# Standing PSUM banks for three projections, and two pieces of tile work placed one iteration later, in a fused attention and expert-lookup kernel

## The chip, the cores and the metric

The kernel runs on one core of one Trainium2 chip. The metric is device time in microseconds of one execution; the number for a kernel is the median of several executions. The core has five engines with a queue each: the Tensor engine (PE, with its weight loads shown apart as PEld), the Vector engine (DVE), the Scalar engine (ACT), GpSimd (POOL) and SyncE (SP), which here only issues DMAs. Each engine works through its own queue in program order; semaphores hold an instruction until what it needs is there.

## The reference

Two branches over the same 2048 tokens of width 512 (32 heads, 16 features) are mixed by a gate:

```python
# A: linear attention with a softmax feature map
qkv = (x @ wqkv)...                                  # q, k, v per head
pq, pk = q @ w_phi, k @ w_phi                        # per head, 16 x 16
phi_q = concat(softmax(pq), softmax(-pq)); phi_k likewise
kv = sum_s phi_k^T v;  z = sum_s phi_k
o = (phi_q @ kv) / (phi_q @ z + 1e-6);  a = o @ wo
# B: 256 experts as 16 x 16, the best one per head
q = x @ w_q;  s1 = q1 @ k1^T;  s2 = q2 @ k2^T        # 16 scores each
e = argmax(s1) * 16 + argmax(s2)                     # top 1, so its softmax is 1
b = sum_h gelu(x . u[e]) * v[e]
# gate
g = sigmoid(x . gate_w);  out = g * a + (1 - g) * b
```

## The kernel before, in words

The tokens are cut into 16 tiles of 128. A matmul of two float32 operands is made of three of a shorter type, high by high, high by low and low by high (`mm3`, lines 52 to 61; the matmuls of lines 57, 59, 60 and 61), over four blocks of the contraction, so twelve matmuls per projection.

Three projections of a tile have 512 columns of which the last 32 are exactly zero, because the last of the 16 features (or score rows) of every head was subtracted from all others: `pq`, the features of q (`front_q`), and `s`, the scores of the first and the second half (`front_s`, half 0 and 1). They are run with `rest=480`: the first matmul of a group writes all 512 columns, so that the 32 zero columns are in the bank, and the other eleven write 480. A fourth projection, `pp` (258 columns, `front_p`), gives the products with u and the gate.

PSUM has eight banks of 512 float32: four with the tag `mm` (`mm_bank`), which every projection, the output `po` of odd tiles and some small results are given in turn, three with the tag `tr` for transposed results, and one with the tag `acc`, first for the sums over k and v (`kvacc`), then for `po` of even tiles.

A first phase over the 16 tiles computes v and the softmax features of k and adds them up in `acc` (`vproj`, `kproj`, `kvacc`); it leaves the work of tiles 14 and 15 partly to the second phase. The second phase is written out by hand in the order in which each engine's queue gets it. Its loop (`for a in range(NT - 2)`, iterations 0 to 13) does for tile a, with the next tile n = a + 1 and older ones:

- PE: `pq` of a (`front_q`); the output of tile a-3 (`push`, `pop`: `po`, 18 matmuls of line 661); the mask of a (`mid_mask`, `mk`: eight small matmuls that read `et`); `oT` of a-2 (`mid_num`, reads `kvb`); both score halves of n; `pp` of n.
- DVE: the softmax of `pq` (lines 117 to 123), with steps of the expert counting woven in (`count`, lines 579 to 613; tile 15's steps come from `step(last, ...)`); sums (472, 476); `best` of n, the equality with the row maximum (lines 504 and 505), for each half.
- ACT: copies, exponentials of the softmax (`soft_exp`, line 462), transposition planes, the output's copy `ot` (line 684).
- GpSimd: products such as `w` (line 468).
- SP: `turn_eq` (line 511) transposes `eq` of n by DMA into `et`, which the mask of the next iteration reads.

In iteration 1 the loop also does both score halves of tile 15, v of tile 14, `best`, `et` and the mask of tile 15. In iteration 2 it does v of tile 15, ends the sums with `kvacc` of 14 and 15, copies them to `kvb` (`kv_final`, line 724), and splits the output weights wo into `wbh` (ACT, lines 820 and 825) and `wbl` (line 861, two blocks on DVE and two on GpSimd). After the loop come tiles 14 and 15, written out; the output of tile 15 goes in two halves through banks `poA` and `poB`.

Of the kernel before, what the change touches and what calls it, by code (L numbers as in the profile page):

```python
# [9 lines left out]
F32 = mybir.dt.float32  # L10
# [24 lines left out]
def mix_kernel(ctx, tc, xT, wqT, wkT, wv, wphi, wo, wq, kk, ug, ev, cst, out):  # L35
# [13 lines left out]
        act.copy(hi, src)  # L49
        eng.tensor_tensor(lo, src, hi, op=ALU.subtract)  # L50

    def mm3(o, pairs, first=True, last=True, rest=None):
        n = len(pairs)
        o_, r = o[:, :rest] if rest else o, slice(0, rest)
        for i, (ah, al, bh, bl) in enumerate(pairs):
            if first and i == 0:
                pe.matmul(o, ah, bh, start=True, stop=False)  # L57
            else:
                pe.matmul(o_, ah, bh[:, r], start=False, stop=False)  # L59
            pe.matmul(o_, ah, bl[:, r], start=False, stop=False)  # L60
            pe.matmul(o_, al, bh[:, r], start=False, stop=(last and i == n - 1))  # L61
# [43 lines left out]
        for k in range(NK):  # L105
            pe.matmul(o[:, :n], xs(t, k)[0], wl[:, k, c0:c0 + n], start=False, stop=(k == NK - 1))

    def proj(o, t, wh, wl, c0, c1, ks=range(NK), rest=None):
        mm3(o, [(*xs(t, k), wh[:, k, c0:c1], wl[:, k, c0:c1]) for k in ks], ks[0] == 0, ks[-1] == NK - 1, rest)

    by_head = lambda a: a.rearrange("p (f h) -> p h f", f=F)

# [146 lines left out]
        pool.tensor_tensor(cols(sl), t3, cols(sh), op=ALU.subtract)  # L259

    st8 = {t: {} for t in range(NT)}

    def front_s(t, half, ks=range(NK)):
        e = st8[t]
        if ks[0] == 0:
            e[half] = mm_bank(f"s{half}_{t}")
        if t == 0 and half == 1:
            return low_last(e[half], t, sh, sl, 512, NR)
        proj(e[half], t, sh, sl, 512 * half, 512 * half + 512, ks, rest=NR)

    pool.memset(warm, 0.0)
    tab = w1.tile([P, 1], F32, bufs=1, name="tab")
# [130 lines left out]
        while t in chains:  # L403
            step(t)

    def front_p(t, evict=True):
        pp = st8[t]["pp"] = mm_bank(f"pp{t}")
        proj(pp[:, :NU], t, uh, ul, 0, NU)
        if evict:
            gelu_pre(t)  # L410
# [29 lines left out]
        pool.tensor_tensor(px, x2, px, op=ALU.mult)  # L440

    def front_q(t):
        pq = mm_bank(f"pq{t}")
        proj(pq, t, wah, wal, 0, D, rest=NR)
        st8[t]["pq"] = pq

    def soft_in(t, step=lambda: None):
# [59 lines left out]

    def turn_eq(t):
        e = st8[t]
        e["et"] = w3.tile([P, 8, P], BF16, tag="eqT", bufs=1, name=f"et{t}")  # L510
        sp.dma_start_transpose(e["et"], e["eq"])

    def mid_phi(t):
# [57 lines left out]
    def count(t, o):  # L571
        e = st8[t]
        i = 2 if t == NT - 1 else t % 2
        A, B = sa[i], sb[i]
        bor = ALU.bitwise_or
        act.copy(A[:, :, 8:24], o.rearrange("p (g a) -> p g a", a=F))
        yield True
        yield True
        yield dve.tensor_tensor(B[:, :, 8:24], A[:, :, 8:24], A[:, :, 7:23], op=bor)
        yield dve.tensor_tensor(A[:, :, 8:24], B[:, :, 8:24], B[:, :, 6:22], op=bor)  # L580
        yield dve.tensor_tensor(B[:, :, 8:24], A[:, :, 8:24], A[:, :, 4:20], op=bor)
        yield dve.tensor_tensor(A[:, :, 8:24], B[:, :, 8:24], B[:, :, 0:16], op=bor)
        m1 = w3.tile([P, 32, 2], U16, tag="m1", name=f"m1{t}")
        m2 = w3.tile([P, 32], U16, tag="m2", name=f"m2{t}")
        twice = lambda a: a.unsqueeze(3).to_broadcast([P, 2, F, 2])
        dve.tensor_tensor(m1.rearrange("p (w a) j -> p w a j", a=F), twice(A[:, 0:2, 8:24]), twice(A[:, 0:2, 7:23]),
                          op=ALU.bitwise_xor)
        yield dve.tensor_tensor(m2.rearrange("p (w a) -> p w a", a=F), A[:, 2:4, 8:24], A[:, 2:4, 7:23],
                                op=ALU.bitwise_xor)
        if t == NT - 1:  # L590
            X = w4.tile([P, 2 * NX], U16, tag="Xl", bufs=1, name=f"X{t}")
        else:
            X = w3.tile([P, 2 * NX], U16, tag="X", bufs=1, name=f"X{t}")
        T = (w4 if t == NT - 1 else w3).tile([P, 2 * NX], U16, tag="Tl" if t == NT - 1 else "T", bufs=1, name=f"T{t}")
        x32, t32 = X.bitcast(U32), T.bitcast(U32)
        srl, band = ALU.logical_shift_right, ALU.bitwise_and
        m1w = m1.rearrange("p a b -> p (a b)").bitcast(U32).rearrange("p (w a) -> p w a", a=F)
        m2w = m2.bitcast(U32).rearrange("p (w b) -> p w b", b=8)
        yield dve.tensor_tensor(x32.rearrange("p (w a b) -> p w a b", w=2, b=8),
                                m1w.unsqueeze(3).to_broadcast([P, 2, F, 8]),  # L600
                                m2w.unsqueeze(2).to_broadcast([P, 2, F, 8]), op=band)
        yield dve.tensor_scalar(t32, x32, 1, 0x55555555, op0=srl, op1=band)
        yield dve.tensor_tensor(X, X, T, op=ALU.subtract)
        yield dve.tensor_scalar(t32, x32, 2, 0x33333333, op0=srl, op1=band)
        yield dve.tensor_single_scalar(x32, x32, 0x33333333, op=band)
        yield dve.tensor_tensor(X, X, T, op=ALU.add)
        yield dve.tensor_tensor(T[:, :NX], X[:, :NX], X[:, NX:], op=ALU.add)
        yield dve.tensor_scalar(x32[:, :NX // 2], t32[:, :NX // 2], 4, 0x0F0F0F0F, op0=srl, op1=band)
        yield dve.tensor_single_scalar(t32[:, :NX // 2], t32[:, :NX // 2], 0x0F0F0F0F, op=band)
        yield dve.tensor_tensor(X[:, :NX], X[:, :NX], T[:, :NX], op=ALU.add)  # L610
        e["C"] = T.bitcast(F32) if t == NT - 1 else w3.tile([P, NX], F32, tag="cf", name=f"cf{t}")
        x8 = X[:, :NX].bitcast(U8).rearrange("p (n b) -> p n b", b=2)
        yield dve.tensor_tensor(e["C"], x8[:, :, 0], x8[:, :, 1], op=ALU.add)
# [19 lines left out]
        act.copy(ch, tj)  # L633
        e["c"] = (ch, cl, tj)

    def back_c(t):
        e = st8[t]
        o = mm_bank(f"CT{t}")
        for j in range(2):
            pe.matmul(o[:, j * P:(j + 1) * P], e["C"][:, j * P:(j + 1) * P], ident, start=(j == 0), stop=(j == 1),  # L640
                      is_transpose=True, skip_group_check=True)
        ch = w4.tile([P, 2 * P], F32R, tag="ch", name=f"ch{t}")
        cl = w4.tile([P, 2 * P], F32R, tag="cl", name=f"cl{t}")
        act.copy(ch, o[:, :2 * P])
        e["c"] = (ch, cl, o)
# [4 lines left out]

    queue, ended = [], []

    def push(t, low_last=False):
        e, h = st8[t], {}

        def mm(lhs, rhs, first=False, last=False):
            def go():
                if first:
                    h["po"] = e["po"] = (psum.tile([P, 512], F32, tag="acc", name=f"po{t}") if t % 2 == 0 else
                                         mm_bank(f"po{t}"))  # L660
                pe.matmul(h["po"], lhs(), rhs, start=first, stop=last)  # L661
                if last:
                    ended.append(t)
            return go
# [108 lines left out]
    def dealt(a, b, z):  # L773
        def first():
            for _ in gate(a):
                step(b)
            step(b, 4)
            if z >= 0:
                back_cl(z)

        def second():
            step(b, 5)
            if 2 < a:
                step(last, 2 if a < 7 else 1)

        moves = iter((first, second, lambda: step(b, 2), lambda: None))
        return lambda: next(moves)()

    for a in range(NT - 2):
        n, b, z, y = a + 1, a - 1, a - 2, a - 3  # L790
        B, Z, Y = b >= 0, z >= 0, y >= 0
        if B:
            planes(b, 0)
            if Z:
# [3 lines left out]
        if a == 1:  # L798
            front_s(last, 0)
            front_s(last, 1)  # L800
            v14 = vproj(NT - 2)
        if a == 2:
            v15 = vproj(NT - 1)
            v15()
            kvacc(NT - 2)
# [8 lines left out]
            for _ in gate(a):  # L814
                pass
        gelu_act(a)
        if a == 2:
            kv_final()
            for k in range(2):
                act.copy(wbh[:, k, :], rawo[k])  # L820
        if a > 0:
            soft_exp(a)
        if a == 2:
            for k in range(2, NK):
                act.copy(wbh[:, k, :], rawo[k])
        if a == 1:
            v14()
        if Y:
            push(y, True)
            pop(18)  # L830
            store_ended()
        if a > 0:
            mid_mask(a)
        if a == 2:
            front_s(n, 0)
# [34 lines left out]
            c_planes(b)  # L870
        if a == 1:
            front_s(n, 1)
            mid_mask(last)
            front_p(n, False)
        soft_b(a)
        if a == 1:
# [6 lines left out]
        if a == 5:  # L883
            neg = w2.tile([P, P], F32R, name="neg", bufs=1)
            act.activation(neg, ident, AF.Copy, scale=-1.0)
        if a == 1:
            step(last, 2)
    a, b, z = NT - 2, NT - 3, NT - 4
    planes(b, 0)
    c_join(z)  # L890
    planes(b, 1)
    front_q(a)
    front_p(last, False)
    gelu_in(a)
    gelu_out(b)
    num_lo(z - 1)
# [2 lines left out]
    coef(b)  # L899
    gelu_act(a)  # L900
    gelu_pre(last)
    push(z - 1, True)
    pop(10)
    mid_mask(a)
    mid_num(z)
# [6 lines left out]
    join(b, 1)  # L912
    mid_num(b)
    store_ended()
    back_c(b)
    front_q(last)
    soft_w(a)
    soft_sum(a, 0)
# [10 lines left out]
    moves = iter((lambda: None, lambda: num_lo(b), lambda: None, lambda: None))  # L929
    soft_in(last, lambda: next(moves)())  # L930
    back_cl(b)
    push(b)
    pop(8)
    mid_phi(a)
    soft_exp(last)
# [1 line left out]
    mid_num(a)  # L937
    pop(6)
    store_ended()
    back_c(last)  # L940
    soft_w(last)
    soft_sum(last, 0)
    soft_sum(last, 1)
# [7 lines left out]
    pop(6)  # L951
    ch, cl, ct = st8[last]["c"]
    low_part(ct[:, :256], ch, cl)
    poA, poB = mm_bank("poA"), mm_bank("poB")
    pA, pB = poA[:, :256], poB[:, :256]
    cA, cB = slice(0, 256), slice(256, 512)
    last_ch(last, pA, cA)
# [8 lines left out]
    last_hi(last, pA, cA)  # L966
    num_low(last)
    last_hi(last, pB, cB)
    back_c(a)
    back_cl(a)  # L970
    last_lo(last, pA, cA)
    ot = w3.tile([P, D], F32, tag="ot", bufs=4, name=f"ot{last}")
# [61 lines left out]
```

## Time and profile before

| | us |
|---|---|
| median of 3 runs | 370.67 (370.65 to 372.22) |
| profiled execution | 370.32 |
| its span, first to last instruction | 368.5 |
| PE busy in the span | 361.6 (98%) |
| DVE busy | 313.5 (85%) |
| ACT busy | 239.2 (65%) |
| GpSimd busy | 160.9 (44%) |
| granted PE clock | 1.000 |

A row of the timeline gives start, duration, engine, line, operation, output and inputs with their tile names, shape and count; in brackets stands how long the engine sat idle before it and what released it. Matmuls are pipelined: the distance from one start to the next is shorter than the duration shown. The chain that ended last follows the work back from the last instruction, at each step to what released it.

### The profile page before, as it was taken

The numbers are of one execution on the slowest core, as the hardware profiler recorded it, in microseconds if no ns is written. First come the engines' busy times: TensorE is split into PE (matmuls) and PEld (weight loads), VectorE is DVE, ScalarE is ACT, GpSimd is POOL, SyncE is SP. The second block draws the span as 40 slices with busy tenths as digits, with TensorE's granted clock in tenths as the row PEclk, the third lists the DMA queues.
The fourth block names the chain that finished last, engine by engine and source line by source line (L and its number), as shares of the span: only waits on it lengthen the run. The fifth ranks groups of instructions, "written<-read, shape, count | busy, mean of one in ns | idle before, by whom it ended". The sixth has DMA issues, their size and how long they took to land.

```text
span 368.5 us, 8817 instructions
## 1 busy us (share of the span) xinstructions
PE 361.6 (98%) x3512; PEld 289.8 (79%) x3512; DVE 313.5 (85%) x729; ACT 239.2 (65%) x440; POOL 160.9 (44%) x171
## 2 busy tenths in 40 slices
PE   7999999999999999999999999999999999999995
PEld 3767787787777878878788888788888888888874
DVE  2459898866859979989999999999999999999783
ACT  4444557635638454586696596696786876879552
POOL 2204365426323833519345364373363463454730
PEclk9999999999999999999999999999999999999999
DMA  8949987487491018440541433626524514445101
GB/s 250 410 156 367 276 246 242 141 249 240 97 296 31 6 27 122 121 87 17 87 109 50 100 82 77 101 59 99 102 44 109 102 49 85 110 49 102 57 31 57
DMA packets 71673, 46.49 MB, mean 126 GB/s; under 512 B 63184, under 2 KB 63824, under 8 KB 69328
## 3 DMA queue, kind: packets, MB, share of 16 engines
q1 hardware_dynamic: 70768, 45.17, 47.4%
q10 hardware_dynamic: 864, 0.76, 0.8%
q8 instruction: 27, 0.44, 0.5%
q14 instruction: 14, 0.11, 0.1%
HBM read 26.39 MB, written 4.19 MB: 83 GB/s over the span
## 4 chain that ended last, share of the span: by engine, by line
PE 93%; DVE 3%; DMA 2%; ACT 1%; issue 0%; SPq 0%; DVEq 0%
PE po L661 16%; PE s L61 7%; PE s L60 7%; PE s L59 5%; PE ws L241 4%; PE pk L61 4%; PE pk L60 4%; PE pq L60 4%; PE pq L61 4%; PE pv L61 4%; PE pv L60 3%; PE pk L59 3%; PE pq L59 3%; PE pv L59 3%; PE s L57 3%; PE oT L547 2%
## 5 line engine op out<-in xcount | busy, mean ns | idle before, releaser
L468 POOL TENSOR_TENSOR w<-d,zb 128x512 f32<-128x512 f32 x32 | 41.3, 1312 | 81.8 <-ACT d L462 79.5
L218 POOL TENSOR_TENSOR d<-d,st 128x1024 f32<-128x1024 f32 x16 | 31.1, 1943 | 60.3 <-DVE st L217 60.3
L61 PE MATMUL s<-sh,xl 128*128 128x480 f32 x124 | 46.9, 378 | 0.0
L60 PE MATMUL s<-sl,xh 128*128 128x480 f32 x124 | 46.9, 378 | 0.0
L462 ACT ACTIVATE d<-d 128x512 f32<-128x512 f32 x32 | 19.9, 631 | 38.4 <-DVE d L121 30.5
L496 POOL TENSOR_TENSOR d<-d,st 128x512 f32<-128x512 f32 x30 | 31.3, 1063 | 24.7 <-DVE st L489 21.2
L539 ACT COPY pt<-tp 128x1024 uint16<-128x1024 uint16 x28 | 36.9, 1399 | 0.0
L59 PE MATMUL s<-sh,xh 128*128 128x480 f32 x93 | 35.3, 380 | 0.0
L381 ACT ACTIVATE d<-d 128x1024 f32<-128x1024 f32 x15 | 15.9, 1063 | 28.2 <-DVE d L123 28.2
L528 ACT COPY pl<-d 128x1024 uint16<-128x1024 uint16 x28 | 29.2, 1044 | 2.8 <-POOL d L496 2.8
L61 PEld LDWEIGHTS s<-sh,xl 128*128 128x128 f32 x124 | 23.2, 187 | 4.0
L60 PEld LDWEIGHTS s<-sl,xh 128*128 128x128 f32 x124 | 23.3, 188 | 3.1
L61 PE MATMUL pk<-wah,xl 128*128 128x480 f32 x64 | 24.3, 380 | 0.0
L60 PE MATMUL pq<-wal,xh 128*128 128x480 f32 x64 | 24.3, 380 | 0.0
L60 PE MATMUL pk<-wal,xh 128*128 128x480 f32 x64 | 24.3, 379 | 0.0
L61 PE MATMUL pq<-wah,xl 128*128 128x480 f32 x64 | 24.3, 379 | 0.0
L661 PE MATMUL po<-wbl,xh 128*128 128x512 f32 x60 | 23.7, 394 | 0.0
L661 PE MATMUL po<-wbh,xh 128*128 128x512 f32 x60 | 23.6, 394 | 0.0
L216 DVE TENSOR_REDUCE st<-d 128x64 f32<-128x1024 f32 x16 | 19.5, 1217 | 4.8 <-ACT d L381 4.5
L505 DVE TENSOR_TENSOR eq<-s,mx 128x512 bf16<-128x512 f32 x32 | 22.1, 692 | 1.1
L472 DVE TENSOR_REDUCE st<-d 128x32 f32<-128x512 f32 x32 | 21.4, 681 | 1.8 <-ACT d L462 0.7
L476 DVE TENSOR_REDUCE st<-w 128x32 f32<-128x512 f32 x32 | 20.6, 677 | 2.3 <-POOL w L468 2.2
(240 smaller groups left out, 1061.6 us busy)
## 6 DMA issues: line engine op xcount, KB each, us to landing
wq<-wq SPq DMA_DIRECT2D x16, 1024.0 KB, 7.1
xr<-xT SPq DMA_DIRECT2D x16, 256.0 KB, 5.9
y<-ot SPq DMA_DIRECT2D x15, 256.0 KB, 2.1
rawk<-wkT SPq DMA_DIRECT2D x1, 1024.0 KB, 8.9
rawq<-wqT SPq DMA_DIRECT2D x1, 1024.0 KB, 7.9
rawo<-wo SPq DMA_DIRECT2D x4, 256.0 KB, 4.1
rawu<-ug SPq DMA_DIRECT2D x2, 258.0 KB, 6.5
rawv<-wv ACTq DMA_DIRECT2D x2, 256.0 KB, 5.7
```

What stands on the lines that cost most here:

```text
L59: pe.matmul(o_, ah, bh[:, r], start=False, stop=False)
L60: pe.matmul(o_, ah, bl[:, r], start=False, stop=False)
L61: pe.matmul(o_, al, bh[:, r], start=False, stop=(last and i == n - 1))
L218: pool.tensor_tensor(g64(d), g64(d), b64(st[:, 128:192]), op=ALU.mult)
L468: pool.tensor_tensor(hs(e["w"], i), hs(e["ph"], i), hs(zb, i), op=ALU.mult)
L472: dve.tensor_reduce(pair(e["st"][:, 64:128])[:, :, 1 - i], hs(e["ph"], i), axis=AX.X, op=ALU.add)
L476: dve.tensor_reduce(pair(e["st"][:, 128:192])[:, :, i], hs(e["w"], i), axis=AX.X, op=ALU.add)
L496: eng.tensor_tensor(g64(d)[:, gs_], g64(d)[:, gs_], r[:, gs_].unsqueeze(2).to_broadcast([P, 32, F]), op=ALU.mult)
L505: dve.tensor_tensor(e["eq"][:, 512 * half:512 * half + 512].rearrange("p (h f) -> p h f", f=F), p3, mx.unsqueeze(2).to_broadcast([P, H, F] ...
L528: act.copy(pl, e["ph"][:, halves[i]].bitcast(U16).rearrange("p (c j) -> p j c", j=2))
L539: act.copy(p16[:, :, 4 * i:4 * i + 4, :], e["tp"][i].rearrange("p (j g) n -> p j g n", j=2))
L661: pe.matmul(h["po"], lhs(), rhs, start=first, stop=last)
```

## The change

`mm3` gets a flag `clean`: with it the first matmul of a group, too, writes only the first 480 columns. From iteration 3 on (`own["on"]`) the roles `pq`, `s0`, `s1` and `pp` each take one of the four `mm` banks and keep it (`own_bank`). In the first use of a bank the group is begun with 512 columns, which leaves zeros in the last 32; every later use sets `clean`. That makes 32 first matmuls of 480 columns: 12 of `pq` (tiles 4 to 15), 10 of each score half (tiles 5 to 14). `po` of every tile in the loop now uses the bank of `acc`; after the loop the last outputs and transposed results are given the standing banks by name.

v of tile 14 moves from iteration 1 to iteration 2, behind `pq` of tile 2. The mask of tile 15 moves from the end of iteration 1 to iteration 2, right ahead of the mask of tile 2. For that `et` of tile 15 gets a buffer of its own, in which the counting buffers X and T of tile 15 are laid later. On ACT, `soft_exp` of tile 2 now stands ahead of `kv_final`, and the four `wbh` casts stand together behind the two mask casts. Of tile 15's counting steps the first is at the end of iteration 2 instead of 1, and from iteration 6 on (before: 7) there is one in an iteration, not two.

```diff
-    def mm3(o, pairs, first=True, last=True, rest=None):
+    def mm3(o, pairs, first=True, last=True, rest=None, clean=False):
         n = len(pairs)
         o_, r = o[:, :rest] if rest else o, slice(0, rest)
+        if clean:
+            o = o_
         for i, (ah, al, bh, bl) in enumerate(pairs):
             if first and i == 0:
-                pe.matmul(o, ah, bh, start=True, stop=False)
+                pe.matmul(o, ah, bh[:, r] if clean else bh, start=True, stop=False)
...
+    own = {}
+
+    def own_bank(role, t):
+        if "on" not in own:
+            return mm_bank(f"{role}_{t}"), False
+        old = role in own
+        if not old:
+            own[role] = mm_bank(role)
+        return own[role], old
 
     def front_s(t, half, ks=range(NK)):
-        e = st8[t]
+        e, clean = st8[t], False
         if ks[0] == 0:
-            e[half] = mm_bank(f"s{half}_{t}")
+            e[half], clean = own_bank(f"s{half}", t)
...
-    def front_p(t, evict=True):
-        pp = st8[t]["pp"] = mm_bank(f"pp{t}")
+    def front_p(t, evict=True, role="pp"):
+        pp = st8[t]["pp"] = own_bank(role, t)[0]
...
     def front_q(t):
-        pq = mm_bank(f"pq{t}")
-        proj(pq, t, wah, wal, 0, D, rest=NR)
+        pq, clean = own_bank("pq", t)
+        proj(pq, t, wah, wal, 0, D, rest=NR, clean=clean)
...
     def turn_eq(t):
         e = st8[t]
-        e["et"] = w3.tile([P, 8, P], BF16, tag="eqT", bufs=1, name=f"et{t}")
+        if t == NT - 1:
+            e["et"] = w4.tile([P, 8, P], BF16, tag="last", bufs=1, name=f"et{t}")
+        else:
+            e["et"] = w3.tile([P, 8, P], BF16, tag="eqT", bufs=1, name=f"et{t}")
...
-                    h["po"] = e["po"] = (psum.tile([P, 512], F32, tag="acc", name=f"po{t}") if t % 2 == 0 else
-                                         mm_bank(f"po{t}"))
+                    h["po"] = e["po"] = bank or psum.tile([P, 512], F32, tag="acc", name=f"po{t}")
...
             if 2 < a:
-                step(last, 2 if a < 7 else 1)
+                step(last, 2 if a < 6 else 1)
...
+        if a == 3:
+            own["on"] = True
...
         if a == 1:
             front_s(last, 0)
             front_s(last, 1)
+        if a == 2:
             v14 = vproj(NT - 2)
-        if a == 2:
+            v14()
             v15 = vproj(NT - 1)
             v15()
             kvacc(NT - 2)
...
         gelu_act(a)
-        if a == 2:
-            kv_final()
-            for k in range(2):
-                act.copy(wbh[:, k, :], rawo[k])
         if a > 0:
             soft_exp(a)
         if a == 2:
-            for k in range(2, NK):
+            kv_final()
+            mid_mask(last)
+            mid_mask(a)
+            for k in range(NK):
                 act.copy(wbh[:, k, :], rawo[k])
-        if a == 1:
-            v14()
...
-        if a > 0:
+        if a > 0 and a != 2:
             mid_mask(a)
...
         if a == 1:
             front_s(n, 1)
-            mid_mask(last)
             front_p(n, False)
...
-        if a == 1:
+        if a == 2:
             step(last, 2)
...
-    push(z - 1, True)
+    push(z - 1, True, own["pp"])
...
-    back_c(b)
+    back_c(b, own["s1"])
...
-    poA, poB = mm_bank("poA"), mm_bank("poB")
+    poA, poB = own["s1"], own["pq"]
```

The three places at which instructions stand in another order, or are another size, for the prediction. First PE's queue in iteration 1, behind the second score half of tile 15 (`s`), before: v of tile 14 (`pv`) comes next.

```order
L60 MATMUL s_15_1836<-sl,xh 128x480
L61 MATMUL s_15_1836<-sh,xl 128x480
L57 MATMUL pv_1849<-wbh,xh 128x512
L60 MATMUL pv_1849<-wbl,xh 128x512
L61 MATMUL pv_1849<-wbh,xl 128x512
```

The same place now: the mask of tile 1 follows, and then the scores of tile 2.

```order
L62 MATMUL s_15_1836<-sl,xh 128x480
L63 MATMUL s_15_1836<-sh,xl 128x480
L580 LDWEIGHTS et_1788
L580 MATMUL mk_1880<-wm,et_1788 128x16
L580 LDWEIGHTS et_1788
```

The twelve `pv` matmuls have left this place; they stand behind `pq` of tile 2 now.

Second ACT's queue in iteration 2, before (`d` is the softmax of tile 2, `rawo` the loaded wo, `sa` and `s` the counting buffers that take a mask `mk`).

```order
L724 COPY kvb<-kvacc 32x8x16 x4
L820 CAST wbh<-rawo_1790 128x512
L820 CAST wbh<-rawo_1792 128x512
L462 ACTIVATE d_2117<-d_2117 128x32x16 x2
L825 CAST wbh<-rawo_1932 128x512
L825 CAST wbh<-rawo_1934 128x512
L576 CAST sa_80<-mk_2156 128x4x16
L551 CAST xh<-oT_0_2179 128x256
```

And now:

```order
L473 ACTIVATE d_2106<-d_2106 128x32x16 x2
L736 COPY kvb<-kvacc 32x8x16 x4
L590 CAST s_1585<-mk_2141 128x4x16
L590 CAST sa_80<-mk_2151 128x4x16
L839 CAST wbh<-rawo_1790 128x512
L839 CAST wbh<-rawo_1792 128x512
L839 CAST wbh<-rawo_1917 128x512
L839 CAST wbh<-rawo_1919 128x512
L565 CAST xh<-oT_0_2178 128x256
```

The two exponentials have moved to the front, the casts of both masks ahead of all four `wbh` casts.

Third PE's first matmuls of `pq` in iteration 4, before and now:

```order
L57 MATMUL pq_2481<-wah,xh 128x512
L60 MATMUL pq_2481<-wal,xh 128x480
L61 MATMUL pq_2481<-wah,xl 128x480
L59 MATMUL pq_2481<-wah,xh 128x480
L60 MATMUL pq_2481<-wal,xh 128x480
```

```order
L59 MATMUL pq<-wah,xh 128x480
L62 MATMUL pq<-wal,xh 128x480
L63 MATMUL pq<-wah,xl 128x480
L61 MATMUL pq<-wah,xh 128x480
L62 MATMUL pq<-wal,xh 128x480
```

Only the first has changed, from 512 columns to 480; the tile has no number any more because it is one bank for all.

More of the change, by code (lines that the diff above doesn't have):

```diff
@@ L106, in low_last, with proj @@
             pe.matmul(o[:, :n], xs(t, k)[0], wl[:, k, c0:c0 + n], start=False, stop=(k == NK - 1))
-    def proj(o, t, wh, wl, c0, c1, ks=range(NK), rest=None):
-        mm3(o, [(*xs(t, k), wh[:, k, c0:c1], wl[:, k, c0:c1]) for k in ks], ks[0] == 0, ks[-1] == NK - 1, rest)
+    def proj(o, t, wh, wl, c0, c1, ks=range(NK), rest=None, clean=False):
+        mm3(o, [(*xs(t, k), wh[:, k, c0:c1], wl[:, k, c0:c1]) for k in ks], ks[0] == 0, ks[-1] == NK - 1, rest, clean)
     by_head = lambda a: a.rearrange("p (f h) -> p h f", f=F)
@@ L261, in mix_kernel @@
     st8 = {t: {} for t in range(NT)}
+    own = {}
[6 more added lines that the diff above has]
+        return own[role], old
     def front_s(t, half, ks=range(NK)):
-        e = st8[t]
+        e, clean = st8[t], False
         if ks[0] == 0:
-            e[half] = mm_bank(f"s{half}_{t}")
+            e[half], clean = own_bank(f"s{half}", t)
         if t == 0 and half == 1:
             return low_last(e[half], t, sh, sl, 512, NR)
-        proj(e[half], t, sh, sl, 512 * half, 512 * half + 512, ks, rest=NR)
+        proj(e[half], t, sh, sl, 512 * half, 512 * half + 512, ks, rest=NR, clean=clean)
     pool.memset(warm, 0.0)
@@ L590, in count @@
         if t == NT - 1:
-            X = w4.tile([P, 2 * NX], U16, tag="Xl", bufs=1, name=f"X{t}")
+            X, T = (e["et"].rearrange("p a n -> p (a n)").bitcast(U16)[:, 512 * i:512 * i + 512] for i in range(2))
         else:
             X = w3.tile([P, 2 * NX], U16, tag="X", bufs=1, name=f"X{t}")
-        T = (w4 if t == NT - 1 else w3).tile([P, 2 * NX], U16, tag="Tl" if t == NT - 1 else "T", bufs=1, name=f"T{t}")
+            T = w3.tile([P, 2 * NX], U16, tag="T", bufs=1, name=f"T{t}")
         x32, t32 = X.bitcast(U32), T.bitcast(U32)
@@ L634, in c_join, with back_c @@
         e["c"] = (ch, cl, tj)
-    def back_c(t):
+    def back_c(t, o):
         e = st8[t]
-        o = mm_bank(f"CT{t}")
         for j in range(2):
@@ L651, in mix_kernel, with push @@
     queue, ended = [], []
-    def push(t, low_last=False):
+    def push(t, low_last=False, bank=None):
         e, h = st8[t], {}
@@ L892, in mix_kernel @@
     front_q(a)
-    front_p(last, False)
+    front_p(last, False, "s0")
     gelu_in(a)
@@ L931, in mix_kernel @@
     back_cl(b)
-    push(b)
+    push(b, bank=own["s0"])
     pop(8)
@@ L939, in mix_kernel @@
     store_ended()
-    back_c(last)
+    back_c(last, own["pp"])
     soft_w(last)
@@ L968, in mix_kernel @@
     last_hi(last, pB, cB)
-    back_c(a)
+    back_c(a, own["s0"])
     back_cl(a)
```

## The prediction

> **What bounds the kernel now.** I read the page first: busy shares and the chain that ended last.
>
> ```profile
> span 368.5 us, 8817 instructions
> PE 361.6 (98%) x3512; PEld 289.8 (79%) x3512; DVE 313.5 (85%) x729; ACT 239.2 (65%) x440; POOL 160.9 (44%) x171
> PE 93%; DVE 3%; DMA 2%; ACT 1%; issue 0%; SPq 0%; DVEq 0%
> ```
>
> The Tensor engine (PE) is the bound: it is on 93% of the chain. Nearly all the rest is one stretch in iteration 2 of the tile loop, where the chain leaves PE and runs through ACT, DVE and a DMA. So two things can be won: matmul columns, and that stretch. The windows view, cut from one tile's mask (`mk`) to the next, shows the loop from mask 6 to mask 7 and from mask 7 to mask 8 (columns: stretch, length, then busy time and count of PE, weight loads, DVE, ACT, GpSimd):
>
> ```profile
> 220.96:235.57 14.61, 14.61 (x107) 12.17 (x107) 14.09 (x39) 10.71 (x23) 6.76 (x7) 1.00 0.36 81
> 235.57:250.04 14.47, 14.47 (x108) 12.18 (x107) 13.92 (x41) 11.03 (x24) 6.79 (x7) 1.00 0.50 87
> ```
>
> An undisturbed iteration is 14.47 us, all of it PE, but the Vector engine (DVE) is busy 13.92 of it: it is the next bound, half a microsecond away. The stretch up to mask 7 is 0.14 longer. Now the waits, in the timelines of PE and of SP's queue:
>
> ```profile
> 175.53 1.08 PE L661 MATMUL po<-wbh,xl 128*128 128x512 f32 x4
> 177.53 0.36 PE L566 MATMUL mk<-wm,et 128*128 128x16 bf16 x8 [0.92 <-DMA et<-eq]
> ...
> 191.10 1.08 PE L661 MATMUL po<-wbh,xl 128*128 128x512 f32 x4
> 192.02 0.36 PE L566 MATMUL mk<-wm,et 128*128 128x16 bf16 x8
> ...
> 234.50 1.08 PE L661 MATMUL po<-wbh,xl 128*128 128x512 f32 x4
> 235.57 0.36 PE L566 MATMUL mk<-wm,et 128*128 128x16 bf16 x8
> ```
> ```profile
> 174.71 1.23 SPq L511 DMA_TRANSPOSE et<-eq  x1
> ...
> 218.14 1.23 SPq L511 DMA_TRANSPOSE et<-eq  x1
> ...
> 232.80 1.23 SPq L511 DMA_TRANSPOSE et<-eq  x1
> ```
>
> From the last `po` row to the mask it is 0.92 us where nothing waits (191.10 to 192.02, mask 4), 2.00 at mask 3 and 1.07 at mask 7. So mask 3 stalls PE for **1.08** and mask 7 for **0.15**. Both wait for `et`, the transposed marks of the best scores, which lands about 2.8 after its issue (174.71 to 177.53; 232.80 to 235.57) and is issued as soon as DVE has finished `best`. The first three gaps between issues are 14.48 each on average (43.43 over 3), the last is 14.66: in iterations 3 to 6 DVE, which also has two count steps of tile 15 in each, is no faster than PE.
>
> **The change, part by part.**
>
> *Columns.* 32 first matmuls (12 of `pq`, 10 each of the two score halves) shrink from 512 to 480 columns. The price is the distance from start to start, since ends are modelled:
>
> ```profile
> 150.91 0.38 PE L60 MATMUL s<-sl,xh 128*128 128x480 f32 x1
> 153.08 0.38 PE L61 MATMUL s<-sh,xl 128*128 128x480 f32 x1
> 157.89 0.39 PE L60 MATMUL pv<-wbl,xh 128*128 128x512 f32 x1
> 160.17 0.40 PE L61 MATMUL pv<-wbh,xl 128*128 128x512 f32 x1
> ```
>
> Ten steps each: 0.217 at 480 columns, 0.228 at 512. So 32 x 0.011 = **0.35**. The rows by form set the other end:
>
> ```profile
> L61 PE MATMUL s<-sh,xl 128*128 128x480 f32 x124 | 46.9, 378 | 0.0
> L57 PE MATMUL s<-sh,xh 128*128 128x512 f32 x31 | 13.9, 448 | 0.0
> L57 PE MATMUL pq<-wah,xh 128*128 128x512 f32 x16 | 6.4, 403 | 0.0
> ```
>
> If the whole duration counted: 20 x 0.070 + 12 x 0.025 = 1.7. I take 0.35: the 448 contains score matmuls that follow another kind of matmul, and that switch stays. The low end is 0.25, if the ten that stand behind `oT` gain nothing.
>
> *Banks.* Each role has one bank from iteration 3 on, so a writer waits for last iteration's reader. For `pq`, scores and `pp` these readers sit in the previous iteration, ahead of the mask. The tightest is `po`, now in one bank for every tile:
>
> ```profile
> 183.01 0.57 ACT L684 COPY ot<-po 128x512 f32<-128x512 f32 x1
> 187.86 0.39 PE L661 MATMUL po<-wbh,xh 128*128 128x512 f32 x1
> ```
>
> The copy that empties it ends 4.3 before the next `po` begins. Cost 0; it would begin to cost once ACT were 4.3 later. The last tiles' banks are named anew, but in the same succession of readers.
>
> *v of tile 14 and the masks of tile 15.* PE does the same work in another order, so nothing is won there by itself; what moves is when DVE gets its input. In iteration 2:
>
> ```profile
> 155.02 0.40 PE L57 MATMUL pq<-wah,xh 128*128 128x512 f32 x1
> 157.66 0.39 PE L57 MATMUL pv<-wbh,xh 128*128 128x512 f32 x1
> ```
> ```profile
> 155.92 0.19 DVE L579 TENSOR_TENSOR s<-s 128x64 uint16<-128x64 uint16 x1
> 157.86 0.69 DVE L117 TENSOR_REDUCE st<-pq 128x32 f32<-128x512 f32 x1 [1.75 <-PE pq L61]
> 164.03 0.68 DVE L123 TENSOR_TENSOR d<-st,pq 128x512 f32<-128x512 f32 x1
> 166.12 2.41 DVE L861 TENSOR_TENSOR wbl<-rawo,wbh 128x512 fp32r<-128x512 f32 x2
> 168.46 0.68 DVE L504 TENSOR_REDUCE mx<-s 128x32 f32<-128x512 f32 x1
> ```
> ```profile
> 162.14 1.06 ACT L724 COPY kvb<-kvacc 32x128 f32<-32x128 f32 x4
> 163.22 1.14 ACT L820 CAST wbh<-rawo 128x512 fp32r<-128x512 f32 x2
> 164.27 1.14 ACT L462 ACTIVATE d<-d 128x512 f32<-128x512 f32 x2
> ```
>
> With v14 (12 x 0.228 = 2.7) and mask 15 (0.3 with its switch) gone from ahead of it, `pq` of tile 2 starts at 152.0 and, 2.64 long as now, is done at 154.7. DVE, free at 155.92 since its L579 step moves as well, no longer waits: its softmax ends 1.94 earlier, at 162.8. ACT then does both exps by 163.4, kvb (1.06) by 164.4, the two small mask casts by about 164.6, and only now the casts wbh, the first two by 165.15 and 165.7. DVE's two `wbl` subtractions therefore gain a new wait: DVE is through its sums at 164.1 and stands until 165.15. What the pair then takes has two bounds, the same form at two places:
>
> ```profile
> L50 DVE TENSOR_TENSOR wbl<-rawv,wbh 128x512 fp32r<-128x512 f32 x4 | 2.8, 739 | 6.9 <-ACT wbh L49 6.9
> L861 DVE TENSOR_TENSOR wbl<-rawo,wbh 128x512 fp32r<-128x512 f32 x2 | 2.4, 1243 | 0.0
> ```
>
> At 1243 each (GpSimd at work on `w` beside it, as now) `best` of tile 3 begins at 167.65, 0.8 earlier than 168.46; at 739 each at 166.65, 1.8 earlier. GpSimd's `w` should be over by about 165.4 and its own subtractions wait for the later casts, so I take a lead of 1.2 to 1.6. The Trainium skill's page "SBUF — State Buffer", section "Who interferes with whom", says that a Vector instruction with two SBUF inputs and a GpSimd instruction that reads SBUF lock each other out whole; by that rule the pair would be blocked only for the tail of `w`, the lead would be about 1.6, and the gain the full 1.58 below; the 739 and 1243 ns agree with it.
>
> What that lead V buys: mask 3 needs V of 1.08. After it DVE gives back 0.2 for the moved L579. Mask 6 has no slack today (218.14 + 2.8 against 220.96) and PE will come 1.08 + 3 x 0.035 earlier, so it needs V = 1.4; iteration 6 has one tile-15 step fewer (0.3), which serves mask 7. With V of 1.4 or more the gain is 0.35 + 1.08 + 0.15 = 1.58. With 1.2, PE is 1.0 earlier at mask 6, 1.2 at mask 7, and 22 of the short matmuls (0.24) follow: 1.45. From iteration 7 on DVE is faster than PE, and the end of the program follows PE. **Sum: 1.5.** The profiled execution took 370.32 (span 368.5 and 1.8 around it), the median 370.67; off the former it is 368.8, off the median **369.2 us**.
>
> Mask 15 costs the same 0.2 in its new place, at 161.6, ahead of scores that nobody waits for.
>
> **The rivals.**
>
> *DVE keeps the stretch.* V is 0.8 or less: the wait for wbh and the pair beside GpSimd eat the lead. PE then gains 0.6 at mask 6, 0.8 at mask 7, and 0.24 behind: 1.04, 369.6. For it: the wait is new and certain. Against: GpSimd should be idle there.
>
> *The short matmuls give more.* With 1.7 in place of 0.35 the time is 367.8; with three quarters of that, 368.3. Against it: the distances above.
>
> *Slower: kvb behind the exps.* ACT now copies kvb, on which PE's `oT` of tile 0 waits, after both exps.
>
> ```profile
> 164.93 0.67 PE L547 MATMUL oT<-pt,kvb 64*32 64x128 f32 x32
> ```
>
> By my times kvb and the mask cast are there at 164.6, 0.25 ahead of PE. If DVE's softmax does not move up, L123 ends at 164.7, the second exp at 165.3, kvb and the casts at 166.6, `oT` is 1.7 late, `wbl` starts at 167.2 and `best` is 1.2 late; mask 3 then comes 1.2 later than 177.53, and DVE, with no slack to mask 7, keeps it. Less 0.5 for columns and order: +0.7, 371.4. It decides once the second exp ends after 163.7.
>
> *Nothing moves.* The columns hide behind a wait of the same size, and the stall returns at another mask: 370.5.
>
> **How the numbers follow.** Chances: forecast 0.52, DVE keeps the stretch 0.22, more from the columns 0.12, nothing 0.08, slower 0.06. The range runs from 368.3 (three quarters of the larger column price) to 370.5. A measurement of this kernel tells 0.5%, 1.85 us, from no change: faster means below 368.8. That takes the column case and the best fifth of the forecast: 0.22. Slower means above 372.5, worse than the slow rival's price: 0.03. No change: 0.75.
>
> **What would show it.** In the changed profile: DVE's first reduction of `pq` in iteration 2 with no wait and near 155.9; a wait of DVE for wbh of about 1 us ahead of `wbl`; the stretch from the last `po` to mask 3 at 0.92 to 1.2 in place of 2.00, and mask 7 at 0.92; iterations of 14.43 from the fourth on. Wrong it is if an `oT`, `po` or `pq` matmul shows a wait in its first use of a standing bank, if iterations 4 to 6 stay at 14.6 because `et` is late, or if the short matmuls stand at the same distance as the long ones.

## The result, and the profile after

The changed kernel takes **368.37 us** (median of 6 runs, 368.07 to 368.54); the kernel before, in the same comparison, 370.66 (6 runs, 370.44 to 372.22). The ratio is 0.9925, 95% interval 0.9904 to 0.9946. The prediction was 369.2 with a range of 368.3 to 370.5; it held "no change", within 0.5%, for the likeliest, and the kernel became 0.75% faster.

The page of the changed kernel's profiled execution (368.09 us), its span, busy shares and chain:

```profile
span 366.3 us, 8798 instructions
PE 361.1 (99%) x3512; PEld 289.9 (79%) x3512; DVE 313.2 (86%) x729; ACT 239.7 (65%) x440; POOL 159.9 (44%) x171
PE 97%; DMA 1%; SPq 0%; DVE 0%; ACT 0%; issue 0%
```

The excursion of the chain through DVE, ACT and a DMA is gone: PE is on 97% of it. Two terms can be read off. First, the places at which PE stood (timeline of PE: last `po` row, then the mask, at masks 3, 6 and 7):

```profile
175.18 1.08 PE L673 MATMUL po<-wbh,xl 128*128 128x512 f32 x4
176.10 0.36 PE L580 MATMUL mk<-wm,et 128*128 128x16 bf16 x8
...
218.43 1.08 PE L673 MATMUL po<-wbh,xl 128*128 128x512 f32 x4
219.43 0.36 PE L580 MATMUL mk<-wm,et 128*128 128x16 bf16 x8
...
232.91 1.08 PE L673 MATMUL po<-wbh,xl 128*128 128x512 f32 x4
233.84 0.36 PE L580 MATMUL mk<-wm,et 128*128 128x16 bf16 x8
```

0.92, 1.00 and 0.93: the 1.08 at mask 3 and the 0.15 at mask 7 have gone, and 0.07 is left at mask 6, where `et` is just in time. Second, the pace. The windows view from mask 5 to mask 13 (eight iterations), of the kernel before and of the changed one:

```profile
206.49:322.37 115.88, 115.88 (x849) 97.40 (x849) 111.65 (x311) 87.11 (x171) 54.23 (x56) 1.00 0.41 85
```
```profile
204.96:320.26 115.30, 115.30 (x850) 97.33 (x849) 111.15 (x309) 87.16 (x171) 54.27 (x56) 1.00 0.41 85
```

Without its stall at mask 7 the former runs at 14.466 us an iteration ((115.88 - 0.15) / 8), the latter, without its 0.07 at mask 6, at 14.404: 0.062 an iteration, where 3 x 0.011 = 0.033 was forecast.

From the first mask of the program to its last `po` row (starts 134.08 and 364.19 before, 133.81 and 361.96 after, all in the timeline of PE) it is 230.11 us before and 228.15 after: **1.96 us** is what the change does in the part of the program that it touches. The other 0.3 lies outside. Ahead of mask 0, where the change moves nothing, the profiled executions of the two kernels already lie 0.27 apart (134.08 and 133.81). There PE waits for its first weights, and that wait differs from one execution to the next; it is part of the difference (waits of PE: total, number, longest; before, the changed kernel, and the kernel e12 below):

```profile
PE pv L195 <- DMA rawv<-wv: 1.0, 1, 1.0
```
```profile
PE pv L197 <- DMA rawv<-wv: 0.2, 1, 0.2
```
```profile
PE pv L197 <- DMA rawv<-wv: 1.4, 2, 0.9
```

Mask 0 begins anywhere from 133.73 to 134.51 in the kernels of this study, so the 0.27 is scatter and not the change's work. In the table below the stretch from mask 0 to the last `po` row therefore stands beside the times: it is the finer measure.

### The profile page after: what moved, and what is told of

It is laid out like the page before. It is cut to its first block, busy times and chain, and to the rows that moved or that the text cites. A ratio compares the mean times of both kernels' runs of the same rounds, so it can differ in the third digit from the quotient of the medians.

```text
span 366.3 us, 8798 instructions
## 1 busy us (share of the span) xinstructions
PE 361.1 (99%) x3512; PEld 289.9 (79%) x3512; DVE 313.2 (86%) x729; ACT 239.7 (65%) x440; POOL 159.9 (44%) x171
## 4 chain that ended last, share of the span: by engine, by line
PE 97%; DMA 1%; SPq 0%; DVE 0%; ACT 0%; issue 0%
PE po L673 15%; PE s L62 7%; PE s L63 7%; PE s L61 6%; PE ws L243 4%; PE pq L62 4%; PE pk L63 4%; PE pq L63 4%; PE pk L62 4%; PE pv L63 4%; PE pv L62 3%; PE pk L61 3%; PE pq L61 3%; PE s L59 3%; PE oT L561 3%; PE pv L61 3%
## 5 line engine op out<-in xcount | busy, mean ns | idle before, releaser
L63 PE MATMUL pv<-wbh,xl 128*128 128x512 f32 x56 | 22.0, 393 | 0.0
L62 PE MATMUL pv<-wbl,xh 128*128 128x512 f32 x56 | 21.9, 391 | 0.0
```

## The experiments

Kernels with the same figure under "before" ran on the same chip beside the same runs of the kernel before. "Stretch gain" is what the stretch from mask 0 to the last `po` row (the last `wbh` row of the output, where the bank has another name) is shorter than the 230.11 of before; "pace" is the mean iteration from mask 5 to mask 13, stalls taken in. Both are read from one profiled execution of each kernel; e0, which is the changed kernel again, gives 1.95 where the first gave 1.96. "One run" means that the time is a single run's, without an interval.

| kernel | time | before | ratio (95%) | stretch gain | pace |
|---|---|---|---|---|---|
| e1 order alone | 368.80 | 370.03 | 0.9970 (0.9958 to 0.9981) | 1.34 | 14.466 |
| e2 banks alone, 512 | 370.19 | 370.03 | 1.0002 (0.9993 to 1.0011) | -0.01 | 14.490 |
| e3 banks and 480 | 369.58 | 370.03 | 0.9986 (0.9977 to 0.9995) | 0.47 | 14.448 |
| e4 order and banks, 512 | 369.08 | 370.03 | 0.9971 (0.9960 to 0.9982) | 1.34 | 14.466 |
| e0 the change | 368.39 | 370.17 | 0.9950 (0.9937 to 0.9962) | 1.95 | 14.413 |
| e5 ACT's order back | 369.89 | 370.17 | 0.9997 (0.9987 to 1.0007) | 0.16 | 14.433 |
| e6 v14 back | 370.27 | 370.17 | 0.9997 (0.9988 to 1.0006) | 0.04 | 14.426 |
| e7 all of `pq` 512 | 369.70 | 370.17 | 0.9988 (0.9980 to 0.9997) | 0.40 | 14.540 |
| e8 banks for `pk` too | 369.00 | 370.36 | 0.9968 (0.9957 to 0.9979) | 2.06 | 14.400 |
| e9 one wide matmul mid-group | 369.58 | 370.36 | 0.9978 (0.9968 to 0.9987) | 0.90 | 14.508 |
| e10 480 for `pq` only | 368.47 | 370.36 | one run | 1.52 | 14.453 |
| e11 480 for both scores only | 368.65 | 370.36 | one run | 1.86 | 14.414 |
| e12 480 for score half 0 only | 369.19 | 370.22 | one run | 1.46 | 14.454 |
| e13 480 for score half 1 only | 368.32 | 370.22 | one run | 1.86 | 14.414 |

### Taking the change apart: e1 to e4

e1 is the kernel before with the moves alone (v14, mask 15, ACT's order, the buffers for them); e2 has the standing banks alone; e3 banks and the narrow opening matmuls; e4 moves and banks. The switches:

```diff
 # e2, e4: standing banks, but every group opened with 512 columns
-        return own[role], old
+        return own[role], False
 # e1: no standing banks
-        if a == 3:
-            own["on"] = True
```

> The order of v of tile 14, the masks of tile 15 and ACT's queue as in the change, but PSUM banks and 512-column first matmuls as before. If the moved work did what the prediction says, the stall of 1.08 us at mask 3 goes, and mask 7's 0.15 as well: 1.2 to 1.3 us faster than before. If the gain beyond 1.5 us came from the order (a second effect of the earlier Vector engine, at the end of the program), 1.6 to 2.0 faster. In the profile the stretch from the last po to mask 3 is 0.92 to 1.0.

> The order as before; standing banks from iteration 3, but every group still begins with 512 columns. If only columns and order count: no difference from before, within 0.1 us. If the standing banks themselves help, because the first matmuls carry fewer waits on other banks' users: 0.3 to 0.4 us faster, with iterations of 14.43 us in place of 14.47 after mask 7.

> The order as before; standing banks with 480-column first matmuls. Up to mask 7 the Vector engine sets the pace here, so only the 22 short matmuls behind it can count. At the predicted 0.011 us each: 0.24 us faster, iterations of 14.43. At the 0.022 that the changed profile suggests: 0.45 to 0.5 faster, iterations of 14.40. If the banks and not the columns are the cause, the same as the banks alone.

> The change with standing banks, but every group begins with 512 columns. By the columns theory the 32 short matmuls are worth 0.7 us: this is 0.7 slower than the change, near 369.1, with iterations of 14.47. By the predicted price 0.35 slower, near 368.7. If the banks themselves carry the extra gain, within 0.3 of the change, near 368.6, with iterations of 14.43.

The moves alone give 1.34 in the stretch (1.23 in time), the banks alone nothing (-0.01; 0.16 in time the wrong way, inside the interval), moves and banks together 1.34 again. In e1 the waits behind `et` are gone as in the change:

```profile
175.12 1.08 PE L674 MATMUL po<-wbh,xl 128*128 128x512 f32 x4
176.05 0.36 PE L580 MATMUL mk<-wm,et 128*128 128x16 bf16 x8
```

In e3 the columns give 0.47 and not the 0.62 that they add to e4 in the change (1.96 - 1.34). Its stall at mask 3 stays, since PE there still waits for `et`:

```profile
177.26 0.36 PE L577 MATMUL mk<-wm,et 128*128 128x16 bf16 x8 [0.89 <-DMA et<-eq]
```

and until mask 7 the pace is DVE's, so what PE saves in iterations 3 to 6 it spends waiting. The two terms help each other: in these iterations the lead of DVE is what lets PE use its shorter matmuls.

### What makes the lead: e0, e5, e6

e0 is the change once more, as the yardstick. e5 puts ACT's order of iteration 2 back, e6 the place of v14.

```diff
 # e5, iteration 2 on ACT
-        if a > 0:
-            soft_exp(a)
         if a == 2:
             kv_final()
             mid_mask(last)
-            mid_mask(a)
-            for k in range(NK):
+            for k in range(2):
                 act.copy(wbh[:, k, :], rawo[k])
+        if a > 0:
+            soft_exp(a)
+        if a == 2:
+            for k in range(2, NK):
+                act.copy(wbh[:, k, :], rawo[k])
+            mid_mask(a)
 # e6: v14 in iteration 1 again
-        if a == 2:
             v14 = vproj(NT - 2)
             v14()
+        if a == 2:
```

> The changed kernel as it is, on the chip and in the session of the runs after it. Theory (two terms that add: order 1.2 to 1.3 us, first matmuls of 480 columns 0.65 to 0.7 us): 1.9 to 2.0 us under the kernel before, so 368.1 where the kernel before takes 370.0; iterations of 14.40 us between masks 8 and 13; masks 3 and 7 without a stall. Rival (the 2.29 us of the first comparison are all the change's): 367.7 beside 370.0. Rival (the column term is 0.35 as predicted and the rest of the gain was chance): 368.45 beside 370.0.

> The change, with ScalarE's order of iteration 2 put back as it was: copies of kv, the mask copies of tile 15 and two of the four wbh copies ahead of the two exponentials, the mask copies of tile 2 behind. v of tile 14 stays where the change has it. If the earlier start of tile 2's softmax alone makes the lead: nothing moves, time as the change, mask 3 follows 0.9 us on the po matmul ahead of it. If ScalarE's order is needed too: the second exponential ends at about 165.1 us instead of 163.2, VectorE begins the best heads of tile 3 1.2 to 2 us later than in the change, and mask 3 waits for 0.3 to 1.1 us (po to mask 1.2 to 2.0 us), with time 0.3 to 1.2 us over the change.

> The change, with the 12 matmuls of v of tile 14 back in iteration 1, ahead of pq of tile 2, and its copy there; ScalarE's new order stays. If the place of v14 makes the lead: VectorE waits 1 to 2 us for pq of tile 2 again, the second exponential ends near 165.1, the kv copies behind it end near 166.2 and oT of tile 0 on TensorE, due at 164.6, waits for them 0.8 to 1.5 us; mask 3 stalls too, unless this wait has made up for it: time 1.0 to 2.3 us over the change. If ScalarE's order alone makes the lead: nothing moves, within 0.2 us of the change.

In time e0 gained 1.78 (370.17 to 368.39), between its first case (1.9 to 2.0) and its last (1.55); its stretch, 1.95, and its pace bear out the first, two terms that add.

Either one undone loses the whole of the moves' gain, and more: e5 and e6 are 1.50 and 1.88 us slower than e0, and with their narrow matmuls they gain 0.16 and 0.04 in the stretch, where e3 without any of the moves gained 0.47. In e5, DVE's timeline of iteration 2:

```profile
161.92 0.68 DVE L125 TENSOR_TENSOR d<-st,pq 128x512 f32<-128x512 f32 x1
164.61 1.28 DVE L483 TENSOR_REDUCE st<-d 128x32 f32<-128x512 f32 x2 [2.01 <-ACT d L473]
165.81 2.40 DVE L876 TENSOR_TENSOR wbl<-rawo,wbh 128x512 fp32r<-128x512 f32 x2
168.13 0.68 DVE L515 TENSOR_REDUCE mx<-s 128x32 f32<-128x512 f32 x1
```

`pq` comes early as in the change, but DVE then stands 2.01 for the exponentials, which ACT holds behind the copies. `best` begins at 168.13, against 168.46 before and 166.23 in the change. That is 1.90 later than in the change, inside the 1.2 to 2 that were expected; the `wbl` pair fell beside GpSimd's `w`, as before the change, and took 2.40. Even so e5 lost more than the expected 0.3 to 1.2, because PE waits for `et` at two masks, 3 and 4, where the expectation had only mask 3 (total, number, longest):

```profile
PE mk L580 <- DMA et<-eq: 0.9, 2, 0.5
```

In e6 the other thing expected shows, PE's timeline:

```profile
165.78 0.40 PE L561 MATMUL oT<-pt,kvb 64*32 64x128 f32 x2 [0.72 <-ACT kvb L736]
166.56 0.67 PE L561 MATMUL oT<-pt,kvb 64*32 64x128 f32 x30 [0.39 <-ACT s L590]
```

This is the prediction's *slower* rival, "kvb behind the exps", with its condition met: DVE's softmax does not move up, the second exponential ends at 165.3, and `oT` waits for `kvb` and the mask cast, 1.11 in all. Its price is not met: the rival had `best` 1.2 late and a loss of 0.7, but the `wbl` pair took 1.29 in e6 too, `best` begins at 168.39, and e6 ends level with the kernel before. Neither half of the move is worth anything alone: an earlier v14 makes ACT's new order a loss, and the old order of ACT eats what v14 has freed.

### What a column costs: e7, e9 to e13

The measured 0.062 per iteration was twice the forecast. e7 widens all twelve `pq` matmuls, e9 adds one wide matmul in the middle of each of the three groups to e4, e10 to e13 narrow the opening matmuls of one role or two.

```diff
 # e7
-        proj(pq, t, wah, wal, 0, D, rest=NR, clean=clean)
+        proj(pq, t, wah, wal, 0, D, rest=None if clean else NR, clean=clean)
 # e9, on e4
+            elif mid and i == 2:
+                pe.matmul(o, ah, bh, start=False, stop=False)
 # e10 (e11: != "pq", e12: == "s0", e13: == "s1")
-        return own[role], old
+        return own[role], old and role == "pq"
```

> The change, with all 12 matmuls of pq 512 columns wide on tiles 4 to 15 instead of 480 (the 32 columns more are zeros): 132 matmuls more that are 32 columns wider, and they do not open an accumulation, 12 that do. What does a column cost? At 0.011 us per 32 columns (the step between 480 and 512 seen in running groups): 1.6 us slower than the change, iterations of 14.53 us. At 0.0133: 1.9 us, 14.56. At 0.022 (the price that the opening matmuls showed): 3.2 us, 14.66.

> The change with its opening matmuls 512 wide again (as in the run of order and banks, iterations of 14.467 us), and in addition the seventh matmul of both halves of the scores and of pq 512 wide from tile 3 on: three single wide matmuls among those of 480. If 32 columns cost 0.013 us: iterations of 14.505. If a single wide matmul among narrow ones costs 0.022, as the three opening ones did (14.467 against 14.400): 14.533. Over 12 iterations 0.45 or 0.8 us slower than order and banks (369.1).

> The change, with 480 columns for the opening matmul of pq alone; those of the scores stay 512. If the three opening matmuls share the gain: iterations of 14.445 us. If pq's alone carries the more of it, as the stretches of an iteration read (scores 0.025 for two, pp and pq 0.02 each): 14.427.

> The change, with 480 columns for the opening matmuls of both halves of the scores alone; that of pq stays 512. If the three share the gain: iterations of 14.422 us. If two of the scores are worth their columns and no more: 14.442.

> The change, with 480 columns for the opening matmul of the scores' half 0 alone (it stands behind the 32 small oT matmuls); those of half 1 and pq stay 512. Iterations with all three wide take 14.466 us. If the surplus belongs to the switch from oT: 14.427 (0.039 off). If both halves share it: 14.440. If it belongs to half 1: 14.453.

> The change, with 480 columns for the opening matmul of the scores' half 1 alone, which stands between matmuls of 480 columns; those of half 0 and pq stay 512. If the surplus belongs to the switch from oT ahead of half 0: iterations of 14.453 us. If both halves share it: 14.440. If it belongs to half 1: 14.427.

The windows view from mask 5 to mask 13 of e4 (all three opening matmuls 512), e7, e9, e10, e12, e13 and e11:

```profile
205.74:321.47 115.73, 115.73 (x849) 97.40 (x849) 111.12 (x309) 86.97 (x171) 54.27 (x56) 1.00 0.40 84
```
```profile
205.26:321.58 116.32, 116.32 (x849) 97.29 (x848) 111.47 (x309) 87.02 (x171) 54.25 (x56) 1.00 0.40 85
```
```profile
205.69:321.75 116.06, 116.06 (x850) 97.48 (x849) 111.35 (x309) 86.93 (x171) 54.19 (x56) 1.00 0.39 84
```
```profile
204.94:320.56 115.62, 115.62 (x849) 97.48 (x849) 111.13 (x309) 86.95 (x171) 54.21 (x56) 1.00 0.40 84
```
```profile
205.59:321.22 115.63, 115.63 (x849) 97.58 (x849) 111.26 (x309) 87.02 (x171) 54.17 (x56) 1.00 0.40 85
```
```profile
205.07:320.38 115.31, 115.31 (x849) 97.19 (x849) 111.15 (x309) 87.05 (x171) 54.21 (x56) 1.00 0.41 85
```
```profile
205.44:320.75 115.31, 115.31 (x849) 97.39 (x849) 111.16 (x309) 86.93 (x171) 54.21 (x56) 1.00 0.41 85
```

Read as prices of one matmul's 32 columns. e7: 14.540 less the change's 14.404 is 0.136 over 12 matmuls, 0.011 each. e9: (116.06 - 115.73) / 8 / 3 = 0.0138. The opening one of `pq` (e10): 0.11 / 8 = 0.0137. That of score half 0 (e12): 0.10 / 8 = 0.0125. All four lie near each other and near the forecast's 0.011. The Trainium skill's page "TensorE: Matmul & The Clock Gate", section "Back-to-back issue gap", gives N / 2.4 ns plus 2.5 as the gap of an isolated matmul of N columns at the full clock; an estimate from it is 13.3 ns for 32 columns. These rows, at 11 to 14 ns in a stream with weight loads, lie near that step; the one that follows does not.

The exception is the opening matmul of **score half 1** (e13): with it narrow an iteration is 0.42 / 8 = **0.052** shorter, four times its columns. With it narrow, narrowing half 0 as well gives nothing more (e11, 115.31 again), and `pq` brings the last 0.010 (14.414 to 14.404). So the prices do not add up: half 0 is worth 0.0125 alone and 0 beside half 1. The expectations of e10, e11 and e13 missed this: 14.453, 14.414 and 14.414 are none of the paces that they named.

The timelines of PE show that the 0.052 is not saved at that matmul. From e4 to e13, in the mean of the eight iterations from mask 5 to mask 13, the distance from half 1's opening matmul to the next start falls by 0.011, from 0.224 to 0.213, which is its columns; the twelve matmuls of half 1 together fall only from 2.604 to 2.600. It is the twelve `pp` matmuls behind them, 258 columns wide in both kernels, that go from 1.456 to 1.419, by 0.037; the last 0.013 falls between `po` and the mask. One iteration of each, the first `pp` row and the first `pq` row behind it, e4 and then e13:

```profile
269.81 0.28 PE L59 MATMUL pp<-uh,xh 128*128 128x258 f32 x1
...
271.27 0.40 PE L59 MATMUL pq<-wah,xh 128*128 128x512 f32 x1
```
```profile
268.93 0.28 PE L59 MATMUL pp<-uh,xh 128*128 128x258 f32 x1
...
270.35 0.40 PE L59 MATMUL pq<-wah,xh 128*128 128x512 f32 x1
```

Half 0's saving is not local either: in e12 its own twelve matmuls take 0.020 less than in e4, half 1's and `pp`'s take 0.019 and 0.012 more, and `pq`'s and the rest 0.013 less each. In the change, with all three narrow, the three groups give 0.039 of the 0.062 against the kernel before, `pp` 0.015 and the rest of the iteration 0.007. So the distance behind a matmul does not tell what an iteration gains when it is narrowed. e9 speaks against one explanation, that any single wide matmul among narrow ones costs extra; e4 against e1 rules out the banks. Why `pp` runs faster behind a narrow half 1 is not shown by these runs and stays open.

### A further step that did not pay: e8

```diff
+        if t < 2:
+            pks[t] = psum.tile([P, 512], F32, tag="mk", bufs=2, name=f"pk{t}")
+        pk = pks[t % 2]
-        proj(pk, t, wah, wal, 0, D, rest=NR)
+        proj(pk, t, wah, wal, 0, D, rest=NR, clean=t > 1)
```

> The change, and in the first phase two standing banks for pk as well, whose first matmul is then 480 columns wide on tiles 2 to 15: 14 opening matmuls. They lie between matmuls of 512 columns of pv and start 0.22 to 0.23 us before the next one. If 32 columns cost 0.013 us wherever they stand (the last run): pairs of tiles take 13.93 us instead of 13.95 there, and the time is 0.18 us under the change. If an opening matmul of 512 costs 0.022: 13.91 us, 0.31 us under. If something else than TensorE sets this phase, 13.95 and no gain.

In the first phase it does what it should. From an opening `pk` matmul to the one eight tiles later, in e0 and in e8 (timelines of PE):

```profile
38.72 0.39 PE L59 MATMUL pk<-wah,xh 128*128 128x512 f32 x1
...
94.54 0.39 PE L59 MATMUL pk<-wah,xh 128*128 128x512 f32 x1
```
```profile
38.34 0.38 PE L63 MATMUL pk<-wah,xh 128*128 128x480 f32 x1
...
94.02 0.38 PE L63 MATMUL pk<-wah,xh 128*128 128x480 f32 x1
```

55.82 against 55.68, 0.0175 for each of eight matmuls, between the two prices expected. But two banks bound to `pk` change the turn in which the other two are given out, and between the phases a score matmul now waits for ACT's reading of another result, which the same matmul in e0 does not:

```profile
132.90 0.50 PE L63 MATMUL s<-sh,xh 128*128 128x512 f32 x1 [0.51 <-ACT zb L764]
```

From `pk` of tile 15 (111.44 in e0, 110.92 in e8) to mask 0 (133.84, 134.33) e8 is 1.01 slower, half of it this wait (the rest was not traced), and it ends 0.6 behind the change, 369.00 beside 368.39, in another comparison on another chip. No kernel here is clearly better than the change itself; e13's 368.32 is a single run, and its stretch is 0.1 longer.

## Why the prediction was right or wrong

**The bound and the stall: right.** Mask 3 and mask 7 lost their waits. The moves were to bring 1.08 + 0.15 = 1.23 and brought 1.34 in e1.

**The lead V: mechanism right, two sizes off that nearly cancel.** V was put at 1.2 to 1.6; `et` of tile 3 is issued 2.21 earlier (SP's queue, 174.71 before):

```profile
172.50 1.23 SPq L525 DMA_TRANSPOSE et<-eq  x1
```

DVE's rows of iteration 2 in the changed kernel:

```profile
155.65 0.68 DVE L119 TENSOR_REDUCE st<-pq 128x32 f32<-128x512 f32 x1
...
161.80 0.68 DVE L125 TENSOR_TENSOR d<-st,pq 128x512 f32<-128x512 f32 x1
162.40 1.47 DVE L483 TENSOR_REDUCE st<-d 128x32 f32<-128x512 f32 x2
165.02 1.29 DVE L873 TENSOR_TENSOR wbl<-rawo,wbh 128x512 fp32r<-128x512 f32 x2 [1.15 <-ACT wbh L839]
166.23 0.69 DVE L515 TENSOR_REDUCE mx<-s 128x32 f32<-128x512 f32 x1
```

Of the 2.21, 0.27 is the earlier start of this execution (mask 0 at 133.81 and 134.08), so V is 1.94. There is no wait for `pq` (155.65, by the same 0.27 ahead of the predicted 155.92), the new wait for wbh is 1.15 (predicted "about 1"), and the pair takes 1.29 together where even the lower bound was 2 x 0.739. GpSimd's `w` beside it is over 0.2 before the pair begins:

```profile
162.28 2.54 POOL L479 TENSOR_TENSOR w<-d,zb 128x512 f32<-128x512 f32 x2 [6.43 <-ACT d L473]
```

The same pair in e5, where `w` runs from 164.66 for 3.00, takes 2.40. So the prediction's reading of "SBUF — State Buffer", "Who interferes with whom", in the Trainium skill (locked out only for the tail of `w`, V about 1.6, the full gain) was the better side of the two bounds, though still short of 1.94; here `w` is over before the pair begins, so there was no tail.

The lead does not last. The transpose of the next tile's `et`, before and in the changed kernel, and that of tile 6's:

```profile
189.02 1.23 SPq L511 DMA_TRANSPOSE et<-eq  x1
```
```profile
187.55 1.23 SPq L525 DMA_TRANSPOSE et<-eq  x1
...
216.66 1.23 SPq L525 DMA_TRANSPOSE et<-eq  x1
```

Less the 0.27, tile 4's is issued 1.20 earlier and tile 6's 1.21 (218.14 before). DVE gave back 0.74 at once, where the prediction had 0.2 for the counting step that moved. That step, 0.19 long before (155.92), now takes 0.87 and ends with a GpSimd product beside it, at 173.2:

```profile
172.35 0.87 DVE L593 TENSOR_TENSOR s<-s 128x64 uint16<-128x64 uint16 x1
```
```profile
171.08 2.08 POOL L507 TENSOR_TENSOR d<-d,st 128x512 f32<-128x512 f32 x2 [0.83 <-DVE st L500]
```

That the product is what holds the step was not tested. So V was 0.3 to 0.7 better than forecast and what DVE gave back 0.5 worse, and that the stall at mask 6 came to no more than 0.07 is in part luck: a V of 1.2 to 1.6 less 0.74 would have left 0.5 to 0.9 there, where 1.21 was just short. The rival "DVE keeps the stretch" is out all the same.

**The banks at 0: right** (e2; e4 against e1). **"Nothing moves" and "slower": did not happen**, the latter because DVE moved up; e6 shows it where DVE does not.

**The columns: this step failed**, "32 x 0.011 = 0.35". The runs showed 0.62. The step that failed is the one that took the distance from a start to the next for the price of a matmul's columns. For the width itself 0.011 was right, and `pq`'s and half 0's opening matmuls are worth about that when they are narrowed alone. But narrowing half 1's is worth 0.052 an iteration, of which 0.011 falls at the matmul and 0.037 at the `pp` matmuls behind it, whose distances the forecast took as fixed; in the change itself, too, `pp` gives 0.015 of an iteration's 0.062. In the kernel before nothing points to it: the next start behind half 1's opening matmul is 0.228 away in the mean of the same eight iterations, as behind any of 512. Only narrowing it alone (e13) showed it, and its cause stays open. The rival "the short matmuls give more" is not what happened: it priced a score matmul at 0.070 and one of `pq` at 0.025 by their durations, 1.7 in all, and that the measured 368.37 lies close to its 368.3 is chance.

**The sum and the chances.** 1.34 + 0.62 = 1.96 where 1.5 stood: 368.7 in place of 369.2 by the prediction's own way of counting. What was measured as the gain went from 1.78 (e0, against 370.17) to 2.29 (the first comparison, against 370.66): the kernel before itself came out at 370.03, 370.17 and 370.36 in the later ones, and ahead of mask 0 the executions differ by 0.8. The line between "no change" and "faster" lay 1.85 below the kernel before, only 0.35 from the middle of the forecast. That is less than the sum was wrong by (0.46) and about the size of the scatter at the start, so the forecast lay too near the line for 0.75 on "no change". The 1.96 alone crosses the line by 0.1; the 0.33 more that makes 2.29 is chance, and beside e0's runs the gain of 1.78 lies on the other side of it.

## What to carry to other kernels

A move that gives one engine its input earlier pays only if the next queue in the line is put in order too: v14 alone and ACT's order alone were both worth nothing (e5, e6), together 1.34 us. Savings on the engine that sets the pace show only where the second engine has a lead: the same narrow matmuls gave 0.47 without the moves and 0.62 with them. For gains of half a per cent, measure from a point behind the start-up to the end inside the profile, and test the price of a piece by narrowing it one role at a time, since what it saves can show at other instructions behind it, and such prices need not add up.

## What the hardware showed that was not expected

Taking 32 columns from the opening matmul of score half 1 shortens an iteration by 0.052 us, and 0.037 of it shows at the twelve `pp` matmuls behind, which are the same in both kernels; at the other places 32 columns were worth 0.011 to 0.014, and the saving on half 0 vanishes beside half 1's. Two DVE subtractions of one form took 1.29 us together with GpSimd idle for all but the last 0.2, and 2.40 with GpSimd at a product beside them. The wait for the first weights at the start took 0.2, 1.0 and 1.4 us in three executions, as much as a term of this change.
